# A check on softmax denominators, and a general path behind a branch at the end

## The chip, the cores and the metric

The kernel runs on one core of one Trainium2 chip. The metric is the device time of one execution in microseconds (us), the median of several runs. The core has five engines that run side by side, each with a queue of its own: TensorE (PE in the profile; PEld is its loading of weights), VectorE (DVE), ScalarE (ACT), GpSimd (POOL) and SyncE (SP). SyncE issues nearly all transfers.

## The reference

Attention over 8 batches, 12 heads, 448 positions and 64 dimensions, whose softmax has one more term in its denominator, and behind it a gate with a long convolution:

```python
scores = scale * np.matmul(q, k.transpose(0, 1, 3, 2))
m = np.max(scores, axis=-1, keepdims=True)
e = np.exp(scores - m)
attn = e / (np.sum(e, axis=-1, keepdims=True) + np.exp(-m) + 1e-09)
attn_out = np.matmul(attn, v)
...
proj = x @ w_proj            # x: the heads side by side, 448 x 768 in each batch
x1, x2, x3 = (proj[..., :D].copy(), proj[..., D:2 * D].copy(), proj[..., 2 * D:].copy())
x2_conv = np.fft.irfft(np.fft.rfft(x2, n=S, axis=1) * H, n=S, axis=1)
y = x1 * x2_conv * x3
return (y @ w_out).astype(np.float32)
```

q, k and v are normal numbers of deviation 0.1, so the scores are near 0. Without the maximum, a denominator is the sum of exp(score) over 448 keys, plus 1.

## The kernel before

The kernel computes exp(score) without subtracting the maximum, in bf16. Two heads (a head pair, 6 in a batch, 48 in all) are done at a time. `attention(i)` adds the work of head pair i: scores in four key tiles on TensorE (L772, L774), exponentials on ScalarE (L785, L791), and the product with v on TensorE (L803, L811). The matrix of v has a column of ones, so the product's last column is the denominator. `norm` on VectorE (L819 to L831) adds 1 to it, takes the reciprocal into the small tile `rec` (128 queries x 2 heads x 4 query tiles), and multiplies the product by it into `xb`. `xb` goes to `xT` by a transposing DMA (`x_dma`, L893) or, in the first batch, through TensorE (`x_pe`).

`dense(b)` adds the work behind the attention of batch b: the folds of `xT` on VectorE (L957, L962), the projection of x2 (`proj2`, L985), the transforms (L1012, L1026, L1032, L1097), the gate projections on TensorE (`gate`, L1058) whose products VectorE forms (L1073), and the output projection (`project`, L1170) with its copy on ScalarE (L1182) and the store from SyncE's queue (L1189, L1192). The dense stage of one batch runs beside the attention of later ones.

The order of every queue is set by `Plan`. Each piece of work is a task: an engine, a cost in us, a due time, what it needs and makes, and what buffers it takes and gives. `Plan.run` goes through the time of a model, lets each engine that is free start the first task in the order of due times that is ready, gives PSUM banks to those that take one, and then emits the instructions in the order found. Costs and due times are constants (`ATT`, `SLOT`, `DENSE`, `PACE` and others). Between plan times 3 and 36 gaps of TensorE are filled with idle matmuls (L1256). A task added for one engine can so alter the order on all. Nothing follows `plan.run()` but the program's end, which the profile gives as line 1335: SyncE waits for all that is out, and the engines meet twice.

```python
add("DVE", 1.03, w - 0.5, norm,
    need=[("V", i, u) for u in range(2)] + ([("X", NHP * (b - 1) - 1)] if b >= 2 else []),
    make=[("xb", i)], give=[("op", i)])
```

Of the kernel before, what the change touches and what calls it, by code (L numbers as in the profile page):

```python
# [23 lines left out]
NHP = H // 2  # L24
SCALE = 1.0 / float(np.sqrt(DH))
# [4 lines left out]
SX = 512  # L30
REM = S - 3 * 128
# [10 lines left out]
class Plan:  # L42
# [26 lines left out]
    def add(self, eng, cost, want, emit, need=(), make=(), take=(), give=(), dma=0.0, run=256, n=1, after=0.0, begun=(), late=0.0):  # L69
        self.tasks.append((want, len(self.tasks), eng, cost, emit, need, make, take, give, dma, after, run, n, begun, late))  # L70
# [186 lines left out]
def kernel(  # L257
# [11 lines left out]
    nc = tc.nc  # L269
# [20 lines left out]
    const = ctx.enter_context(tc.tile_pool(name="const", bufs=1))  # L290
# [16 lines left out]
    wproj_bf = wts.tile([128, NDT, 3 * D], BF16, name="wproj_bf")  # L307
    wout_bf = wts.tile([128, NDT, D], BF16, name="wout_bf")
    hrs = wts.tile([FQ, 2, 2, D], BF16, name="hrs")
# [24 lines left out]
    nf = nat.bitcast(F32)  # L334
# [3 lines left out]
    def stage(g, at, n):  # L338
# [4 lines left out]
    plan = Plan(  # L343
        {
            "e": 6, "er": 2, "k0": 2, "q0": 2, "u": 1, "w": 1, "xf": 1,
            "x2": 1, "xs": 2, "t0": 2, "t1": 2, "yh": 1, "g": 1, "x1": 2, "cr": 2, "cw": 1, "cv": 2, "yT": 1, "yR": 1,
            "os": 3,
        }
    )
    add = plan.add  # L350

    psum = psp.tile([128, 8 * 512], F32, name="psum")
    psum2 = psum.bitcast(BF16)
# [354 lines left out]
    W = {}  # L708
# [51 lines left out]
    def attention(i):  # L760
        b, hp = divmod(i, NHP)
# [31 lines left out]
        def out_banks():  # L793
            return pair(("op", i))[:, :, 0 : NST * (DH + 1)].rearrange("p u (n d) -> p u n d", n=NST)
# [24 lines left out]
        def norm():  # L819
            op = out_banks()  # L820
            if ("xb", b) not in W:
                W["xb", b] = xbp.tile([128, NHP, NST, 128], BF16, name="xb")
            rec = small.tile([128, 2, NST], F32, name="rec")
            nc.vector.tensor_scalar_add(rec, op[:, :, :, DH], 1.0)  # L824
            nc.vector.reciprocal(rec, rec)
            nc.vector.tensor_tensor(  # L826
                W["xb", b][:, hp].rearrange("p n (u d) -> p u n d", u=2),
                op[:, :, :, 0:DH],
                rec[:].unsqueeze(3).to_broadcast([128, 2, NST, DH]),
                op=ALU.mult,  # L830
            )  # L831
# [14 lines left out]
        for t in range(4):  # L846
            w = tau(i, t / 4 if i or t else 1.0)
            ex = with_rests(i - 1) if t == host else dict(cost=0.0, emit=lambda: None, need=[], make=[], take=[], give=[])
            if t == 0 or b == 0:

                def one(t=t, ex=ex):
# [4 lines left out]
                    need=[("kT", i), ("qT", i)] + ([("S", i - 1, 2)] if b else []) + ([] if i or t else ["kT0"]) + ex["need"]  # L856
                    + ([("S", i, t - 1) if t > 1 else ("S", i - 1, 3)] if t and (i or t > 1) else []),
                    make=[("S", i, t)] + ex["make"], take=[(ring(t), ("S", i, t))] + ex["take"], give=ex["give"])
            elif (3 * i + t) % 2 == 0:
# [3 lines left out]
                def both(pair=(old, (i, t)), ex=ex):  # L863
# [5 lines left out]
                    need=[("kT", old[0]), ("qT", old[0]), ("kT", i), ("qT", i)] + ex["need"]  # L869
                    + [("S", old[0], old[1] - 1) if old[1] > 1 else ("S", i - 1, 3)],  # L870
                    make=[("S",) + old, ("S", i, t)] + ex["make"],
                    take=[("sc", ("S",) + old), ("sc", ("S", i, t))] + ex["take"], give=ex["give"])
            add("ACT", 0.81 if t else 0.44, w - 1.0, lambda t=t: exps(t), need=[("S", i, t)],
                make=[("e", i)], take=[("e" if t else "er", (i, t))], give=[(ring(t), ("S", i, t))])
        if i == n_batches * NHP - 1:
            ex = with_rests(i)
            add("PE", 0.19 + ex["cost"], tau(i, 1.1), out_rests, need=ex["need"], make=ex["make"], take=ex["take"],
                give=ex["give"])

        w = tau(i + 1, (2 if i % 2 else 1) / 4) + 0.01  # L880
        for u in range(2):
            add("PE", 0.385, w + 0.01 * u, lambda u=u: out_rest(u), need=[("ER", i)], make=[("V", i, u)],
                take=[("op", i)], give=[("e", (i, t)) for t in range(1, 4)])
        add("DVE", 1.03, w - 0.5, norm,
            need=[("V", i, u) for u in range(2)] + ([("X", NHP * (b - 1) - 1)] if b >= 2 else []),
            make=[("xb", i)], give=[("op", i)])

        def xT():
            if ("xT", b) not in W:
# [26 lines left out]
        w = tau(i, 1.7)  # L916
        on_act = 4 <= i < 6
        old = [("G", b - 2)] if b >= 2 else []
        if b in XALL or b > 1 and hp < NHP - 1:
            if hp in (2, NHP - 1 if b in XALL else NHP - 2):  # L920
                ps = range(0, 3) if hp == 2 else range(3, hp + 1)
                add("SP", 1.3, w, x_dma, need=[("xb", NHP * b + h) for h in ps] + old,
                    make=[m for h in ps for m in (("X", NHP * b + h), ("xT", b, h))], dma=0.5 * len(ps), late=1.2)
# [309 lines left out]
                O(st, ch)  # L1233


    E = mybir.EngineType
    with (
        tc.tile_pool(name="tabs", bufs=1) as tp,
        tc.manual_schedule(engines={E.PE, E.Pool, E.DVE, E.Activation, E.SP}),
    ):  # L1240
        zero1 = tp.tile([128, 1], F32, name="zero1")
        warm = tp.tile([128, 1], F32, name="warm")
        add("DVE", 0.1, -20.0, lambda: nc.vector.memset(zero1, 0.0), make=["zero1"])
        add("POOL", 1.1, -20.0, count, make=["count"])
        add("POOL", 0.6, -19.0, lambda: make_identity(nc, ident_bf), make=["ident"])
        first = tp.tile([1, 16], BF16, name="first")
        add("POOL", 3.4, -18.5, lambda: nc.gpsimd.dma_start(first, moe_w_out[0:1, 0:16]), need=["ident"], dma=0.05)
        add("DVE", 0.2, -19.5, number, need=["count"], make=["row"])
        add("DVE", 2.6, -19.0, phases, need=["row"], make=["phases"])

        idle = tp.tile([128, 128], BF16, name="idle")
        add("DVE", 0.15, -19.9, lambda: nc.vector.memset(idle, 0.0), make=["idle"])

        def fill(i, count):
            for _ in range(count):
                nc.tensor.matmul(psum[:, 512 * i : 512 * i + 128], idle, idle)  # L1256

        plan.fill = fill

        def spin():  # L1260
# [25 lines left out]
        for b in range(n_batches):  # L1286
            if b < NSTAGED:
                staged(b)
            else:
                loaded(b)  # L1290
        add("DVE", 0.5, tau(NHP * NSTAGED) - 30.0, lambda: nc.vector.memset(kn[:, :, 0, :], 0.0),
            need=[("c" + x, g) for x in "kqv" for g in range(NHP * NSTAGED - NHP, NHP * NSTAGED - 2)], make=["zero kn"])
        for (part, ch), at in zip(LOADS, LOAD):
            if part == "F":
                add("POOL", 1.6, at, filter_load, need=["ft", "bps"], make=["filt"], take=[("yT", "F")], dma=4.1, run=1500, n=3, after=at)
            elif part == "O":
                add("POOL", 0.95, at, wout_load, make=["wout"], dma=6.9, run=1500, after=at)
            elif ch is None:
                add("POOL", 0.95, at, lambda part=part: wproj_load(part, None), make=[("w", part, 0), ("w", part, 1)], dma=6.9,
                    run=1500, after=at)  # L1300
            else:
                add("POOL", 0.7, at, lambda part=part, ch=ch: wproj_load(part, ch), make=[("w", part, ch)], dma=3.5, run=1500, after=at)
        more_tables()
        filter_spectrum()
        for i in range(n_batches * NHP):
            attention(i)
        for b in range(n_batches):
            dense(b)
        plan.run()


# [28 lines left out]
```

## Time and profile before

| what | value |
|---|---|
| time, median of 3 runs | 386.22 us (385.4 to 386.39) |
| span of the profiled execution, first to last instruction | 384.4 us |
| what lies around the span, from the three times | 1.0 to 2.0 us |
| TensorE busy | 364.9 us, 3700 matmuls |
| VectorE busy | 261.8 us, 667 instructions |
| ScalarE busy | 264.1 us, 460 instructions |
| GpSimd busy | 112.2 us, 240 instructions |
| mean granted TensorE clock | 0.998 |

The page has no other time of the profiled execution than its span, so its own time is read as the span and what the three times leave around it. A row of instructions has the line, the engine, the operation, output and input tiles, their shapes, the count, the busy time, and the idle time of the engine just before them with what ended it. A row of the windows has a stretch, its length, the busy time and count of TensorE, weight loads, VectorE, ScalarE and GpSimd, then the granted clock, the share of the DMA engines, and GB/s. A row of waits has who waited for whom, the sum, the number of times and the longest. A q behind an engine's name is its queue. An issue of a DMA is on its queue's engine; its landing is later.

### The profile page before, as it was taken

What the parts mean: (1) busy time and instruction counts of PE and PEld (TensorE: products, weight loads), DVE (VectorE), ACT (ScalarE), POOL (GpSimd) and SP (SyncE); (2) the same over time, 40 slices, a digit from 0 to 9 for tenths busy, and PEclk for the clock granted to TensorE, in tenths of its full rate; (3) what the DMA queues carried; (4) which work ended last, traced back from release to release, by engine and by line L of the source; (5) the groups of instructions that cost most, each with busy time, mean ns of one, the idle gap of its engine ahead of it and who ended that gap; (6) DMA issues with size and microseconds to landing.
All of it is one profiled execution on the core that took longest, in us unless ns stands there. A gap on an engine that the chain in (4) does not pass through costs nothing.

```text
span 384.4 us, 9536 instructions
## 1 busy us (share of the span) xinstructions
PE 364.9 (95%) x3700; PEld 232.4 (60%) x3700; DVE 261.8 (68%) x667; ACT 264.1 (69%) x460; POOL 112.2 (29%) x240
## 2 busy tenths in 40 slices
PE   7887799999998999889989999999999999999995
PEld 6555575557654676545755666565665567667553
DVE  6575758996868357997596576665488725987660
ACT  5698487884885868767756658886778587444543
POOL 5692436141835533445552411110000000000000
PEclk9999999999999999999999999999999999999999
DMA  8999998599999999999999933592302132200214
GB/s 207 265 225 232 249 219 197 131 178 218 262 269 273 249 261 244 263 230 251 247 241 226 274 112 100 102 210 96 84 3 43 41 124 43 43 1 2 82 41 165
DMA packets 116333, 64.43 MB, mean 168 GB/s; under 512 B 73085, under 2 KB 112704, under 8 KB 116288
## 3 DMA queue, kind: packets, MB, share of 16 engines
q1 hardware_dynamic: 111568, 58.18, 63.5%
q0 software_dynamic: 4480, 5.41, 8.3%
q8 instruction: 29, 0.48, 0.5%
q10 hardware_dynamic: 240, 0.23, 0.3%
q14 instruction: 16, 0.13, 0.1%
HBM read 43.86 MB, written 11.01 MB: 143 GB/s over the span
## 4 chain that ended last, share of the span: by engine, by line
PE 65%; DVE 13%; DMA 12%; ACT 4%; issue 2%; POOL 2%; SPq 2%; POOLq 0%; DVEq 0%; ACTq 0%
PE psum L1058 19%; PE psum L985 14%; PE psum L1170 12%; PE psum L811 6%; PE psum L772 5%; DMA nat<-in_k_dram 5%; DMA xT<-xb 3%; DVE t L1026 2%; DMA nat<-in_v_dram 2%; PE psum L1097 2%; PE psum L1012 2%; DMA nat<-in_q_dram 2%; DVE xf L962 2%; DVE yh L1032 2%; ACT e L785 2%
## 5 line engine op out<-in xcount | busy, mean ns | idle before, releaser
L785 ACT ACTIVATE e<-psum 128x896 bf16<-128x896 f32 x144 | 126.4, 925 | 21.8 <-PE psum L772 21.6
L1058 PE MATMUL psum<-xT,wproj_bf 128*128 128x448 bf16 x576 | 122.4, 352 | 0.1
L1058 PEld LDWEIGHTS <-wproj_bf 128*128 128x128 bf16 x576 | 53.5, 97 | 42.8 <-issue 1.3
L985 PE MATMUL psum<-wproj_bf,xf 128*113 128x384 bf16 x384 | 69.1, 326 | 1.5 <-DVE g L1073 0.7
L985 PEld LDWEIGHTS <-xf 128*113 128x113 bf16 x384 | 50.0, 132 | 15.3 <-issue 3.4
L1170 PE MATMUL psum<-wout_bf,yT 128*128 128x384 bf16 x288 | 52.9, 326 | 0.0
L811 PE MATMUL psum<-vn,e 128*128 128x65 bf16 x1152 | 44.7, 194 | 0.0
L1070 ACT CAST x<-psum 128x448 bf16<-128x448 f32 x48 | 25.6, 534 | 25.8 <-PE psum L1058 24.5
L1026 DVE TENSOR_TENSOR t<-xs,hrs 113x768 bf16<-113x768 bf16 (+1 forms) x64 | 37.0, 613 | 8.0 <-ACT xs L1020 8.0
L772 PE MATMUL psum<-qT,kT 64*128 64x448 bf16 x288 | 40.8, 355 | 0.6 <-ACT kT L485 0.4
L1182 ACT COPY osb<-psum 128x384 f32<-128x384 f32 x56 | 26.4, 484 | 21.3 <-PE psum L1170 20.0
L811 PEld LDWEIGHTS <-e 128*128 128x128 bf16 x1152 | 39.2, 97 | 2.8
L568 POOL CAST nat<-nat 112x512 bf16<-112x512 f32 x36 | 24.1, 671 | 52.6 <-DMA nat<-in_q_dram 49.2
L1170 PEld LDWEIGHTS <-yT 128*128 128x128 bf16 x288 | 27.5, 98 | 19.2 <-issue 1.5
L824 DVE TENSOR_SCALAR rec<-psum 128x8 f32<-128x8 f32 x48 | 7.7, 161 | 44.8 <-PE psum L811 44.3
L1073 DVE TENSOR_TENSOR g<-x,psum 128x448 bf16<-128x448 bf16 x48 | 29.5, 615 | 11.9 <-PE psum L1058 9.5
L999 ACT CAST x<-psum 113x384 bf16<-113x384 f32 x32 | 15.5, 483 | 28.7 <-PE psum L985 28.5
L826 DVE TENSOR_TENSOR xb<-psum,rec 128x512 bf16<-128x512 f32 x48 | 33.2, 691 | 1.7
L1020 ACT CAST xs<-psum 113x384 bf16<-113x384 f32 (+1 forms) x64 | 28.2, 499 | 3.8 <-PE psum L1012 3.6
L1106 ACT CAST cr<-psum 128x452 bf16<-128x452 f32 x48 | 25.3, 547 | 7.0 <-PE psum L1097 6.6
L791 ACT ACTIVATE er<-psum 128x448 bf16<-128x448 f32 x48 | 26.7, 556 | 4.6 <-PE psum L774 4.6
L997 DVE CAST x<-psum 113x384 bf16<-113x384 f32 x32 | 17.5, 550 | 14.1 <-PE psum L985 14.1
(111 smaller groups left out, 435.7 us busy)
## 6 DMA issues: line engine op xcount, KB each, us to landing
nat<-in_q_dram SPq DMA_DIRECT2D x47, 224.0 KB, 4.7
out_dram<-osb SPq DMA_DIRECT2D x24, 384.0 KB, 2.4
nat<-in_k_dram SPq DMA_DIRECT2D x41, 192.0 KB, 4.9
nat<-in_v_dram SPq DMA_DIRECT2D x41, 192.0 KB, 4.9
wproj_bf<-in_moe_w_proj_dram POOLq DMA_DIRECT2D x2, 1152.0 KB, 17.3
rests<-in_k_dram SPq DMA_DIRECT2D x8, 192.0 KB, 4.9
rests<-in_v_dram SPq DMA_DIRECT2D x8, 192.0 KB, 5.2
out_dram<-osb SPq DMA_DIRECT2D x8, 192.0 KB, 2.9
```

Of the source, the lines that this page charges most:

```text
L772: nc.tensor.matmul(sc[:, u, 0:S], kT[b % 2][c, hp, t, :], qT[b % 2][c, hp, :])
L785: nc.scalar.activation(to, of, AF.Exp, scale=SCALE)
L791: nc.scalar.activation(to, of, AF.Exp, scale=SCALE)
L811: nc.tensor.matmul(out_bank(u)[:, n, :], P["e"][1 + t][:, u * S + n * 128 : u * S + n * 128 + 128], vn[b % 2][:, hp, 4 * u + t, :], start= ...
L826: nc.vector.tensor_tensor(W["xb", b][:, hp].rearrange("p n (u d) -> p u n d", u=2), op[:, :, :, 0:DH], rec[:].unsqueeze(3).to_broadcast([1 ...
L985: nc.tensor.matmul(pps[:FQ, :DCH], W["xf", b][:, pg, kt, 0:FQ], wproj_bf[:, kt, D + ch * DCH : D + (ch + 1) * DCH], start=(kt == 0), stop= ...
L1020: nc.scalar.copy(L["xs", par, ch][:K, pg % 2, :], L["Z", pg, ch][:K, :DCH])
L1026: nc.vector.tensor_tensor(t[:K], L["xs", par, ch][:K], h, op=ALU.mult)
L1058: nc.tensor.matmul(p[:, :S], wproj_bf[:, kt, 2 * part * D + dt * 128 : 2 * part * D + (dt + 1) * 128], xT()[:, kt, 0:S], start=(kt == 0), ...
L1073: nc.vector.tensor_tensor(g[:, dt, :], L["x1", dt], p[:, :S], op=ALU.mult)
L1170: nc.tensor.matmul(ops[:n, :DCH], y[:, dt, 0:n], wout_bf[:, dt, ch * DCH : (ch + 1) * DCH], start=(dt == 0), stop=(dt == NDT - 1),)
L1182: nc.scalar.copy(L["os", st][:n, ch * DCH : (ch + 1) * DCH], L["O", st, ch][:n, :DCH])
```

## The change

`norm` writes the denominators' reciprocals into a buffer of the batch (`dens`, one of two) that is kept. After the last head pair of a batch VectorE takes the minimum of it with `low`, a running minimum that starts at 1. After all batches, `judge` reduces `low` over its free axis and compares it with 1/65536; a matmul with a column of ones sums the 128 marks, and VectorE copies the sum to `flag` as an integer. All of these are tasks of the plan. Behind `plan.run()` the flag is loaded into a register of each engine, and where it is over 0 a general path (`stable`) recomputes the attention with the maximum in f32 for each batch, and `dense` runs again for it with a plan of its own. No constant of the planner is altered.

```diff
--- before.py
+++ after.py
@@ -349,6 +349,13 @@
     )
     add = plan.add
 
+    LARGE = 65536.0
+    dens = [const.tile([128, NHP, 2, NST], F32, name=f"den{i}") for i in range(2)]
+    low = const.tile([128, NHP, 2, NST], F32, name="low")
+    one = const.tile([128, 1], BF16, name="one")
+    bad = const.tile([128, 1], BF16, name="bad")
+    flag = const.tile([1, 1], I32, name="flag")
+
     psum = psp.tile([128, 8 * 512], F32, name="psum")
     psum2 = psum.bitcast(BF16)
 
@@ -820,7 +827,7 @@
             op = out_banks()
             if ("xb", b) not in W:
                 W["xb", b] = xbp.tile([128, NHP, NST, 128], BF16, name="xb")
-            rec = small.tile([128, 2, NST], F32, name="rec")
+            rec = dens[b % 2][:, hp]
             nc.vector.tensor_scalar_add(rec, op[:, :, :, DH], 1.0)
             nc.vector.reciprocal(rec, rec)
             nc.vector.tensor_tensor(
@@ -882,8 +889,11 @@
             add("PE", 0.385, w + 0.01 * u, lambda u=u: out_rest(u), need=[("ER", i)], make=[("V", i, u)],
                 take=[("op", i)], give=[("e", (i, t)) for t in range(1, 4)])
         add("DVE", 1.03, w - 0.5, norm,
-            need=[("V", i, u) for u in range(2)] + ([("X", NHP * (b - 1) - 1)] if b >= 2 else []),
+            need=[("V", i, u) for u in range(2)] + ([("X", NHP * (b - 1) - 1), ("low", b - 2)] if b >= 2 else []),
             make=[("xb", i)], give=[("op", i)])
+        if hp == NHP - 1:
+            add("DVE", 0.12, w + 3.0, lambda: nc.vector.tensor_tensor(low, low, dens[b % 2], op=ALU.min),
+                need=[("xb", NHP * b + h) for h in range(NHP)] + ["low"], make=[("low", b)])
 
         def xT():
             if ("xT", b) not in W:
@@ -1232,6 +1242,78 @@
             for ch in range(2):
                 O(st, ch)
 
+
+    def watch():
+
+        def fresh():
+            nc.vector.memset(low, 1.0)
+            nc.vector.memset(one, 1.0)
+
+        def judge():
+            worst = small.tile([128, 1], F32, name="worst")
+            nc.vector.tensor_reduce(worst, low[:].rearrange("p g u n -> p (g u n)"), axis=mybir.AxisListType.X, op=ALU.min)
+            nc.vector.tensor_single_scalar(bad, worst, 1.0 / LARGE, op=ALU.is_lt)
+
+        last = ("low", n_batches - 1)
+        hy = ("hy", "flag")
+        add("DVE", 0.15, 20.0, fresh, make=["low"], after=12.0)
+        add("DVE", 0.35, tau(NHP * n_batches, 4.0), judge, need=[("low", b) for b in range(n_batches)], make=["bad"])
+        add("PE", 0.1, tau(NHP * n_batches, 4.0), lambda: nc.tensor.matmul(bank(hy)[0:1, 0:1], bad, one), need=["bad"],
+            make=["count bad"], take=[hy])
+        add("DVE", 0.1, tau(NHP * n_batches, 4.0), lambda: nc.vector.tensor_copy(flag, bank(hy)[0:1, 0:1]), need=["count bad"],
+            make=["flag"], give=[hy])
+
+    def stable(b):
+
+        at = [0]
+
+        def room(*shape):
+            n = int(np.prod(shape[1:]))
+            t = nf[0 : shape[0], at[0] : at[0] + n]
+            at[0] += n
+            return t.rearrange("p (a c) -> p a c", a=shape[1]) if len(shape) > 2 else t
+
+        eye = room(128, 128)
+        qa, ka, va = (room(SP, NST, DH) for _ in range(3))
+        qt, kt = (room(DH, S) for _ in range(2))
+        ex, et = room(128, S), room(SP, NST, 128)
+        top, neg, off, den = (room(128, 1) for _ in range(4))
+        area = [psum[:, 512 * i : 512 * i + 512] for i in range(8)]
+        nc.vector.tensor_copy(eye, ident_bf)
+        W["xb", b] = x = xbp.tile([128, NHP, NST, 128], BF16, name="xb")
+        W["xT", b] = xt = xtp.tile([128, NDT, SX], BF16, name="xT")
+        nc.vector.memset(x[:, :, NST - 1, :], 0.0)
+        for h in range(H):
+            hp, u = divmod(h, 2)
+            for to, of in ((qa, q), (ka, k), (va, v)):
+                nc.sync.dma_start(to, of[b, h].rearrange("(t p) d -> p t d", p=SP))
+            for i, (of, to) in enumerate(((qa, qt), (ka, kt))):
...
+            for n in range(NST):
+                m = 128 if n < 3 else REM
+                sc = area[2][0:m, 0:S]
+                nc.tensor.matmul(sc, qt[:, n * 128 : n * 128 + m], kt)
+                nc.vector.tensor_reduce(top[0:m], sc, axis=mybir.AxisListType.X, op=ALU.max)
+                nc.vector.tensor_scalar(neg[0:m], top[0:m], -SCALE, None, op0=ALU.mult)
+                nc.scalar.activation(ex[0:m], sc, AF.Exp, scale=SCALE, bias=neg[0:m])
...
+        for hp in range(NHP):
+            for t in range(NST):
+                nc.tensor.transpose(psum2[:, 1024 * 5 + t * 128 : 1024 * 5 + (t + 1) * 128], x[:, hp, t, :], ident_bf)
+            nc.vector.tensor_copy(xt[:, hp, 0:S], psum2[:, 1024 * 5 : 1024 * 5 + S])
 
     E = mybir.EngineType
     with (
@@ -1306,7 +1388,24 @@
             attention(i)
         for b in range(n_batches):
             dense(b)
+        watch()
         plan.run()
+
+    overflow = nc.values_load(flag[0:1, 0:1], min_val=0, max_val=128)
+    with (
+        tc.If(overflow > 0),
+        tc.manual_schedule(engines={E.PE, E.Pool, E.DVE, E.Activation, E.SP}),
+    ):
+        W.clear()
+        for b in range(n_batches):
+            stable(b)
+            plan = Plan(plan.size)
+            plan.FILL, add = (0.0, 0.0, 0.0), plan.add
+            ready = ["ft", "bt", "half", "wout", ("hrs", 0), ("hrs", 1), ("y", b - 1, 1)]
+            ready += [("w", n, i) for n in range(3) for i in range(2)] + [("xT", b, h) for h in range(NHP)]
+            add("DVE", 0.01, -100.0, lambda: None, make=ready, after=1.0)
+            dense(b)
+            plan.run()
 
 
 # ---- launch: one core; inputs and outputs as the reference has them ----
```

More of the change, by code (lines that the diff above doesn't have):

```diff
@@ new lines, in stable @@
+    def stable(b):
[21 more added lines that the diff above has]
+                for t in range(NST):
+                    nc.tensor.transpose(area[i][0:DH, t * SP : (t + 1) * SP], of[:, t, :], eye[0:SP, 0:SP])
+                nc.vector.tensor_copy(to, area[i][0:DH, 0:S])
+            for n in range(NST):
[5 more added lines that the diff above has]
+                nc.scalar.activation(ex[0:m], sc, AF.Exp, scale=SCALE, bias=neg[0:m])
+                nc.vector.tensor_scalar(off[0:m], neg[0:m], 88.0, None, op0=ALU.min)
+                nc.scalar.activation(off[0:m], off[0:m], AF.Exp)
+                nc.vector.tensor_reduce(den[0:m], ex[0:m], axis=mybir.AxisListType.X, op=ALU.add)
+                nc.vector.tensor_scalar(den[0:m], den[0:m], off[0:m, 0:1], 1e-9, op0=ALU.add, op1=ALU.add)
+                nc.vector.reciprocal(den[0:m], den[0:m])
+                nc.vector.tensor_scalar(ex[0:m], ex[0:m], den[0:m, 0:1], None, op0=ALU.mult)
+                for t in range(NST):
+                    nc.tensor.transpose(area[3][0:SP, t * 128 : t * 128 + m], ex[0:m, t * SP : (t + 1) * SP], eye[0:m, 0:m])
+                nc.vector.tensor_copy(et[:, :, 0:m], area[3][0:SP].rearrange("p (a c) -> p a c", a=NST)[:, :, 0:m])
+                for t in range(NST):
+                    nc.tensor.matmul(area[4][0:m, 0:DH], et[:, t, 0:m], va[:, t, :], start=(t == 0), stop=(t == NST - 1))
+                nc.scalar.copy(x[0:m, hp, n, u * DH : (u + 1) * DH], area[4][0:m, 0:DH])
+        for hp in range(NHP):
+            for t in range(NST):
+                nc.tensor.transpose(psum2[:, 1024 * 5 + t * 128 : 1024 * 5 + (t + 1) * 128], x[:, hp, t, :], ident_bf)
+            nc.vector.tensor_copy(xt[:, hp, 0:S], psum2[:, 1024 * 5 : 1024 * 5 + S])
```

## The prediction

> **What bounds the kernel now.** I read the summary of engines first, then the windows by stage, then what TensorE waited for, and last the final microseconds.
>
> ```profile
> PE 364.9 (95%) x3700; PEld 232.4 (60%) x3700; DVE 261.8 (68%) x667; ACT 264.1 (69%) x460; POOL 112.2 (29%) x240
> PE   7887799999998999889989999999999999999995
> ```
>
> TensorE is busy for 364.9 of 384.4 us. VectorE has 122.6 us of idle time, so small work on it costs nothing unless TensorE waits for its result. The windows say where TensorE's idle time lies:
>
> ```profile
> 24.00:36.00 12.00, 9.89 (x173) 7.09 (x173) 9.31 (x28) 11.07 (x18) 6.14 (x14) 1.00 1.17 228
> 36.00:50.00 14.00, 10.62 (x131) 7.57 (x130) 9.15 (x25) 8.40 (x12) 6.28 (x11) 1.00 1.17 242
> 150.00:200.00 50.00, 45.95 (x471) 28.04 (x470) 40.54 (x92) 35.21 (x61) 24.80 (x50) 1.00 1.07 249
> 250.00:300.00 50.00, 50.00 (x535) 31.43 (x532) 32.71 (x90) 38.74 (x67) 1.18 (x3) 1.00 0.35 84
> 330.00:360.00 30.00, 30.00 (x188) 19.08 (x187) 24.49 (x66) 13.32 (x29) 0.00 (x0) 1.00 0.11 28
> 360.00:385.00 25.00, 20.53 (x136) 11.91 (x134) 9.18 (x24) 10.40 (x22) 0.00 (x0) 0.95 0.26 95
> ```
>
> The second number is TensorE's busy time in the stretch. From 250 us to the last matmul at 380.56 TensorE is full. It has holes in the first 50 us, and 4.05 us of them between 150 and 200 us. Those last ones come from VectorE; the view of waits, cut to that stretch and engine, names them:
>
> ```profile
> PE psum L1097 <- DVE g L1073: 2.9, 3, 1.2
> PE psum L985 <- DVE g L1073: 0.7, 1, 0.7
> PE psum L803 <- DVE g L1073: 0.5, 1, 0.5
> ```
>
> The end is the part that the change touches most. The timeline of SyncE's queue has the last store; the view of line 1335 (the program's end) has what follows it; the view of line 1189 has the time that a store takes:
>
> ```profile
> 381.07 0.34 SPq L1189 DMA_DIRECT2D out_dram<-osb  x1
> ```
>
> ```profile
> L1335 SPq EVENT_SEMAPHORE  x11: 17/28/28, 381.5 to 384.4; - x11
> L1335 SPq DRAIN  x3: 7/7/7, 383.6 to 383.9; - x3
> L1335 ACTq EVENT_SEMAPHORE  x2: 17/17/17, 383.8 to 384.4; - x2
> ```
>
> ```profile
> DMA to landing us min/median/max: 2.3/2.4/5.5
> ```
>
> So the last store is issued by 381.4, lands 2.3 us after its start (381.07 + 2.3 = 383.4), SyncE's queue drains at 383.6, and two rounds in which the engines meet end the span at 384.4. Closing costs 0.8 us behind the drain, and one round some 0.2 us (drain at 383.6, the others released at 383.8).
>
> The program itself is fetched while it runs, and the page shows it:
>
> ```profile
> q8 instruction: 29, 0.48, 0.5%
> q14 instruction: 16, 0.13, 0.1%
> ```
>
> One packet of q8 is 0.48 MB / 29, some 16 KB, and takes 0.5% x 384.4 x 16 / 29 = 1.06 us; one of q14 is 8 KB and takes 0.1% x 384.4 x 16 / 16 = 0.4 us (0.2 to 0.6 by the rounding).
>
> The sum is made against the profiled execution, whose span is 384.4 us. The three timed runs lie 1.0 to 2.0 us above that span, their median 386.22 us 1.8 us above; I add the change in span to the median. About 0.3% (1.16 us) is what a measurement of this kernel can tell from no change.
>
> **The change part by part.**
>
> Denominators kept in "dens" instead of "rec": the same three instructions with the same shapes (161, 203 and 691 ns at lines 824 to 826). 0.
>
> Eight minima on VectorE, 128x48 f32: nearest rows are the 128x8 f32 TENSOR_SCALAR of 161 ns and the 128x128 bf16 TENSOR_TENSOR of 268 ns (L1141); I take 0.22 us, 1.8 us in all. They lie in VectorE's 122.6 us of idle time. Each stands behind the last normalisation of its batch, so "xb", which the transposing DMA waits for, is not later; what queues behind a minimum is the next copy or gate product. Where that is a product that TensorE waits for (150 to 200 us, line 1073), a minimum moves the matmul by 0.22 us: two batch ends there, at most 0.4 us. I take 0.1.
>
> The two memsets at about 12 us: 59 ns each by the row of "zero", beside 5.2 us of idle VectorE in 12 to 24 us. 0. Without that cover they would cost 0.12.
>
> The judgement: a reduction (about 0.22 us), a comparison (0.15, as the 128x1 TENSOR_SCALARs of L652), and the copy of the flag out of PSUM (0.17, as L824). VectorE is free for 5.5 of the 30 us from 330 on. The reduction waits for the last minimum, in VectorE's own order, so nothing new is late. The copy waits for the one-column matmul; behind it in the queue stand the products of batch 7, delayed by a semaphore's turn of some 0.2 us.
>
> The one-column matmul stands in TensorE's full stretch, so all of its time counts: 24 matmuls of L811 with 65 columns take 0.87 us in the chain of waits, 0.04 each; the longest row for one from start to end is 0.19. I take 0.1. It also waits for "bad", and behind it in TensorE's queue stand the gate matmuls of the last batch (L1058). After 250 us the trace shows no wait of TensorE for VectorE to speak of, but the longest one anywhere for a VectorE result is 1.23 us. So 0.04 to 1.4, taken 0.1.
>
> The planner: new VectorE tasks shift the due times of everything that it sorts from plan time 12 on, and so the orders of all queues. Not shown by any row. Bounds: the 4.05 us of holes from 150 to 200 us close (a gain of 4.1), or as many again open (a loss of 4.1). With TensorE full from 250 us on, any order does the same work, so I take 0 and keep both ends.
>
> The end. Five queues each read the flag into a register, compare, and jump over the general path, which is thousands of instructions long (12 heads x 4 query tiles x some 20 instructions, for 8 batches). None of this is in the trace, so it is bounded.
> Read and compare: below by two queue instructions (0.06 each from one closing wait to the next: 11 of them in the 0.65 us around a landing), above by a store's round trip of 2.3. It is one word, so nearest to what a queue spends on one instruction with addresses, the 0.34 us DMA issue; with the compare I take 0.5.
> The jump: below 0.06 if the target is already there; above a round trip of 2.3 and a 16 KB block of 1.06, 3.4. All that is known of fetching is that a block is a DMA. The 384 KB store moves for some 0.95 us of its 2.4 (about 400 GB/s in its window), so 1.4 us is not transfer; with 0.4 to 1.06 for the block that is 1.8 to 2.5. I take 2.0.
> [...]
> Semaphores: the path not taken must leave them as the other path would, bounded by 0 and by two passes of the closing waits; one pass, 11 x 0.06, is 0.6, which I take.
> Meeting: if the engines meet before the branch (the last store landed, 383.4 and a round of 0.2), nothing of this hides under the store. If they do not, it runs under the 2.0 us between 381.4 and 383.4. I take the meeting, since the general path writes what the fast path still reads, and price its round 0.2; and one more pass of closing waits of 0.4 that no longer hides under the landing.
> Sum of the end: 0.5 + 2.0 + 0.6 + 0.2 + 0.4 = 3.7 us.
>
> Total: 0.1 + 0.1 + 3.7 = 3.9: span 388.3, time 386.2 + 3.9 = 390.1 us, slower by 1.0%. Chance of this forecast, with its own range of 388.7 to 392: 0.43.
>
> **The rivals.**
>
> No meeting: each queue branches when its own work is done. TensorE, VectorE and GpSimd are done by 380.6 and hide everything. SyncE is free at 381.4; 0.5 + 2.0 + 0.6 brings it to 384.5, then 0.6 of waits and 0.8 of closing make 385.9. That is 1.5 more than 384.4, with 0.2 for the rest 387.9 us. For it: nothing in the data needs a meeting when the path is not taken. Chance 0.26.
>
> Hidden, no change: as before, but jump and read together cost SyncE under 2.0 us, the block being there or coming in 0.4. Then only the 0.6 and 0.2 remain: 386.2 to 387.2 us. [...] Chance 0.10.
>
> Faster: the new order closes the holes of 150 to 200 us (L1097, L985 and L803 waiting for the product of L1073). All 4.05 us closed with the unmet end of 1.5 gives 386.2 - 4.05 + 1.7 = 383.9 us. It decides from 2.9 us closed on with that end, and can't with my 3.7. Against it: new tasks on VectorE give it more to do in just that stretch (40.5 of 50 us busy). Chance 0.05.
>
> New waits: the changed order opens 4 us of holes, in the first 50 us or where VectorE is late with a product. 390.1 + 4.1 = 394.2 us. For it: in the first 50 us TensorE is idle 9.3 us and waits for casts, key and query copies and "xb", all of them in queues that the planner reorders. Chance 0.15.
>
> The branch is taken: the eight dense stages run again, whose L1058, L985 and L1170 alone hold 122.4 + 69.1 + 52.9 = 244 us of TensorE, so over 630 us. Denominators are sums of 448 exponentials of numbers near 0, far below 65536. Chance 0.01.
>
> **How the numbers follow.** The prediction is the likeliest, 390.1. The range goes from 386.9 (below the unmet end and the upper edge of the hidden one) to 394.5 (the new waits); out of it fall the faster case, most of the hidden one, and the upper tail, some 0.17. Slower by over 0.3%: 0.43 + 0.26 + 0.15 + 0.01 = 0.85. Within 0.3%: 0.10. Faster: 0.05.
>
> **What would show it.** The end: in the rows of the last 10 us, reads and branches of all five queues behind the landing of the last store, and 3 us or so between branch and closing (met), or between 381 and 384 (unmet). Instruction packets in the last 5 us, one for each engine, show the fetch. The minima: eight of 0.2 us. The matmul: no gap behind it in TensorE's timeline. The planner: TensorE's busy sum stays at 365, and the last matmul's end moves from 380.56 by under 1 us; if that end moves by more, the change's cost is order and not branch, and the forecast is wrong in its reason even where its number holds. A last matmul near 380.7 with a span of 385 would say that the branch hides.

## The result and the profile after

The changed kernel took 390.09 us in the median of 15 runs, against 386.22 before. The ratio to before is 1.0097, with a 95% interval of 1.0074 to 1.0120, so about 3.7 us (2.9 to 4.6) slower. The ratios here leave out executions more than 1.5% above the fastest of their kernel. A second comparison of the same kernel, told below, gave 1.0118 (1.0058 to 1.0179). The forecast was 390.1 us, slower; its reason holds only in part, as told below.

The summary of engines and the windows of the changed kernel, with the same columns as before:

```profile
PE 364.7 (95%) x3701; PEld 232.4 (60%) x3701; DVE 264.6 (69%) x680; ACT 264.3 (69%) x460; POOL 111.5 (29%) x240
```

```profile
150.00:200.00 50.00, 47.28 (x487) 29.01 (x485) 42.03 (x99) 35.62 (x63) 24.14 (x48) 1.00 1.10 248
250.00:300.00 50.00, 50.00 (x504) 30.80 (x502) 33.75 (x95) 37.67 (x66) 0.00 (x0) 1.00 0.31 73
330.00:360.00 30.00, 30.00 (x192) 19.25 (x192) 23.20 (x63) 13.60 (x30) 0.00 (x0) 1.00 0.11 28
360.00:386.00 26.00, 18.27 (x120) 10.55 (x118) 8.66 (x22) 8.83 (x19) 0.00 (x0) 0.94 0.28 95
```

TensorE does one matmul more, VectorE 13 instructions and 2.8 us more. TensorE is full from 250 us on as before, and its holes from 150 to 200 us are still there (2.7 us in this execution). TensorE's waits in the main part are mostly for the same producers as before, and not longer in sum: it is idle for 13.6 us up to its last matmul, against 15.6 before. The end has a new wait. This is the view of what SyncE's queue waited for from 376 us on:

```profile
SPq L1396 <- SPq L1396: 4.3, 1, 4.3
SPq L1434 <- PEq L1434: 0.7, 2, 0.5
```

In the kernel before, the same view has the landing of the store in that place:

```profile
SPq L1335 <- DMA out_dram<-osb: 1.5, 2, 1.0
```

Line 1396 is the branch. SyncE's queue stands still there for 4.3 us, and waits for nothing but itself. The timeline of its queue has the last store, and the views of lines 1394 (the load of the flag), 1396 and 1434 (the closing) show the rest:

```profile
378.81 0.34 SPq L1199 DMA_DIRECT2D out_dram<-osb  x1
```

```profile
L1394 SPq TENSOR_LOAD <-flag x1: 1205/1205/1205, 330.5 to 330.5; - x1
L1394 ACTq TENSOR_LOAD <-flag x1: 673/673/673, 378.3 to 378.3; - x1
```

```profile
L1396 SPq EVENT_SEMAPHORE  x8: 17/17/17, 383.5 to 384.0; - x8
...
L1396 DVEq COMPARE_BRANCH  x1: 72/72/72, 371.9 to 371.9; - x1
L1396 DVEq EVENT_SEMAPHORE  x1: 21/21/21, 374.7 to 374.7; - x1
L1396 PEldq COMPARE_BRANCH  x1: 3426/3426/3426, 375.8 to 375.8; - x1
L1396 ACTq COMPARE_BRANCH  x1: 50/50/50, 379.1 to 379.1; - x1
L1396 SPq COMPARE_BRANCH  x1: 58/58/58, 379.2 to 379.2; - x1
...
L1396 ACTq EVENT_SEMAPHORE  x1: 17/17/17, 383.5 to 383.5; - x1
```

Read it engine by engine, from COMPARE_BRANCH to the EVENT_SEMAPHORE behind it. VectorE branches at 371.9 and goes on at 374.7: 2.8 us. ScalarE branches at 379.05 and goes on at 383.52: 4.4 us behind the branch. SyncE branches at 379.20, and its first instruction past the general path is at 383.51: 4.3 us. GpSimd, which has no work in the general path, goes on 0.13 us behind its branch at 331.8. TensorE's branch takes 3.4 us, but at 375.8 it has that much work queued, and its matmuls run on to 378.27 and hide most of it. The packets of the instruction queues lie in these gaps. The view of DMA queues, cut to 379.2 to 383.5 us:

```profile
q8 instruction: 1, 0.02, 1.3%
q14 instruction: 2, 0.02, 0.9%
```

The two packets of q14, 8 KB each, start 1.8 to 1.9 us behind the branches (381.00 and 381.01), take 0.31 and 0.32 us, and another 2.2 us pass before the two queues go on.

It is best to measure the end from the start of the last store, since the main part of one execution is up to some us longer than that of another. Before: 381.07 to 384.43, a tail of 3.37 us. After: 378.81 to 385.74, 6.93 us. The difference, 3.56 us, is 0.92%, which is all but 0.05% of the measured ratio. The spans alone (384.4 and 385.7) would give 1.3 us, because the profiled execution after had its last store 2.3 us earlier; the next experiment shows that the change has no part in that.

One reason why main parts differ can be read from the traces. In some executions TensorE's granted clock falls to 0.5 for one stretch of 3.4 us within the main part. The kernel without the branch, told next, has one from 39.3 to 42.7 us; its window of 38 to 44 us, with the granted clock as the last number but two, shows it (0.28 of 6 us is 3.4 us at half the clock):

```profile
38.00:44.00 6.00, 4.57 (x51) 3.41 (x52) 3.76 (x9) 2.27 (x3) 4.67 (x9) 0.72 1.14 260
```

Of the 14 traces told here, eight have such a stretch (one of them two), and their last store starts at 381.6 to 382.5 us. The other six, with those of the kernel before and of the changed kernel among them, have none, and it starts at 378.8 to 381.2 us. What sets the spread within the six is not shown.

### The profile page after: what moved, and what is told of

It reads as the page before. It is cut to its first block, busy times and chain, and to the rows that moved or that the text cites. A ratio compares the mean times of both kernels' runs of the same rounds, so it can differ in the third digit from the quotient of the medians.

```text
span 385.7 us, 9576 instructions
## 1 busy us (share of the span) xinstructions
PE 364.7 (95%) x3701; PEld 232.4 (60%) x3701; DVE 264.6 (69%) x680; ACT 264.3 (69%) x460; POOL 111.5 (29%) x240
## 4 chain that ended last, share of the span: by engine, by line
PE 54%; DMA 22%; DVE 8%; SPq 7%; POOL 4%; issue 2%; ACT 1%; POOLq 0%; DVEq 0%
PE psum L1068 17%; PE psum L995 12%; PE psum L1180 11%; DMA nat<-in_k_dram 10%; DMA nat<-in_q_dram 10%; PE psum L818 5%; PE psum L779 4%; SPq L547 3%; PE psum L1107 2%; DVE t L1036 2%; PE psum L1022 2%; DVE yh L1042 1%; DMA xT<-xb 1%; SPq L569 1%; PE psum L781 1%
## 5 line engine op out<-in xcount | busy, mean ns | idle before, releaser
L1036 DVE TENSOR_TENSOR t<-xs,hrs 113x768 bf16<-113x768 bf16 (+1 forms) x64 | 36.1, 599 | 7.3 <-ACT xs L1030 7.3
L818 PEld LDWEIGHTS <-e 128*128 128x128 bf16 x1152 | 39.3, 97 | 2.8
L831 DVE TENSOR_SCALAR den<-psum 128x8 f32<-128x8 f32 x48 | 7.8, 162 | 45.2 <-PE psum L818 44.5
L833 DVE TENSOR_TENSOR xb<-psum,den 128x512 bf16<-128x512 f32 x48 | 33.2, 692 | 1.7
```

Of the source, the lines that this page charges most:

```text
L818: nc.tensor.matmul(out_bank(u)[:, n, :], P["e"][1 + t][:, u * S + n * 128 : u * S + n * 128 + 128], vn[b % 2][:, hp, 4 * u + t, :], start= ...
L833: nc.vector.tensor_tensor(W["xb", b][:, hp].rearrange("p n (u d) -> p u n d", u=2), op[:, :, :, 0:DH], rec[:].unsqueeze(3).to_broadcast([1 ...
L1036: nc.vector.tensor_tensor(t[:K], L["xs", par, ch][:K], h, op=ALU.mult)
```

## The experiments

The tail is everywhere the time from the start of the last store to the end of the span.

**The work without the branch.** From the changed kernel:

```diff
         watch()
         plan.run()
 
-    overflow = nc.values_load(flag[0:1, 0:1], min_val=0, max_val=128)
-    with (
-        tc.If(overflow > 0),
...
```

> The changed kernel with the minima, the judgement, the matmul and the copy of the flag, but without the load of the flag into registers, the branch and the general path behind it. Theory (the end costs all: SyncE's and ScalarE's jumps over the general path, and a longer closing): 386.2 us, the time before, within 0.8, since the orders of the queues are the same but for the added tasks. Rival (the new tasks and the altered order cost it): 388 us or more. Rival (the new work speeds the plan up by 2 us, as the earlier last matmul of the one profile of the changed kernel would have it): 384.2 us.

Measured: 1.0013 of before (0.9983 to 1.0044), tail 3.37 us, exactly that of before. The view of waits of SyncE's queue has the store's landing again as the longest wait of the end, as before:

```profile
SPq L1419 <- DMA out_dram<-osb: 1.5, 2, 1.0
```

Laid side by side with the kernel before, by operation and shape, the work and the DMA issues of ScalarE, GpSimd and SyncE stand in the same order. TensorE's list is the same but for the flag's matmul. VectorE's is the same but for the 13 added instructions up to the 585th of its 667; behind that, a fold and a gate product of the last batch change places. So the planner moved next to nothing, and the 13 instructions cost nothing that can be measured (at most 0.44% by the interval). Both rivals fall, the one that sees a 2 us faster plan as well.

**The branch without the work.** The normalisation before is kept, and the minima are gone (these lines of the edit are left out here); the flag is set by a memset:

```diff
...
-        watch()
         plan.run()
+        nc.vector.memset(flag, 0)
 
     overflow = nc.values_load(flag[0:1, 0:1], min_val=0, max_val=128)
```

> The kernel before with its own normalisation and no judgement; the flag is set to 0 by one memset on VectorE behind its last work, and then the flag is loaded, compared and the same general path jumped over as in the changed kernel. Theory (the end costs all): 386.2 + 3.5 to 4 = 390 us, as the changed kernel, with its wider scatter too. Rival (the new tasks cost it): 386.2 to 387 us.

Measured: 1.0136 (1.0090 to 1.0181), tail 6.44 us; SyncE's jump took 3.8 us, ScalarE's 4.4, VectorE's 2.8. The branch alone costs what the change costs, within the two intervals, and the rival falls. The tail accounts for 0.8% of the 1.36%.

**A near target.** The general path is five instructions, one for each engine:

```diff
-        W.clear()
-        for b in range(n_batches):
-            stable(b)
...
+        nc.vector.memset(low, 1.0)
+        nc.gpsimd.memset(one, 1.0)
+        nc.scalar.copy(dens[0], dens[1])
+        nc.tensor.matmul(psum[0:1, 0:1], bad, one)
+        nc.sync.dma_start(out[n_batches - 1, 383:384, 0:48], dens[0][0:1].rearrange("p g u n -> p (g u n)"))
```

> The changed kernel with a general path of five instructions, one for each engine, in place of the thousands; the condition is the same and the path is not taken. This leaves the recomputation out. Theory (the jump waits for its target to be fetched, 4.3 us on SyncE in the profile of the changed kernel): with a near target the jump takes 0.1 us, SyncE is at its last waits before the store has landed, and the time is 386.2 + 0.5 to 1.0 = 387 us. Rival (a branch costs this wherever it goes, or it is loading the flag): 389 to 390 us.

> The kernel with a general path of five instructions once more (it leaves the recomputation out). Its first comparison gave 1.0057 of before, with a tail (start of the last store to the end of the span) of 3.39 us, the same as before. Theory (only the tail costs): 0.999 to 1.003 of before. Rival (loading and judging the flag costs time that no row of the tail shows): 1.004 to 1.008 again.

Measured: 1.0057 (1.0022 to 1.0092) the first time and 1.0003 (0.9966 to 1.0040) the second, and a tail of 3.39 us both times. The view of the branch's line in the second:

```profile
L1396 ACTq COMPARE_BRANCH  x1: 45/45/45, 382.8 to 382.8; - x1
L1396 SPq COMPARE_BRANCH  x1: 57/57/57, 382.9 to 382.9; - x1
L1396 ACTq EVENT_SEMAPHORE  x1: 17/17/17, 383.0 to 383.0; - x1
L1396 SPq EVENT_SEMAPHORE  x1: 17/17/17, 383.1 to 383.1; - x1
```

SyncE is past the branch 0.2 us after it, and the store's landing ends the kernel as before. So load, comparison and branch are free here, and it is the far target that costs. The first ratio, 388.4 us, lies 1.4 us above the theory's 387, and its interval reaches into the rival's range; the second excludes the rival. I take the tail, which is the same in both, and leave the 1.0057 as unexplained.

**The general path placed aside.**

```diff
-        tc.If(overflow > 0),
+        tc.If(overflow > 0, preferred_fallthrough_block=False),
```

> The changed kernel with the general path placed aside, so that the path not taken goes on behind the comparison and only the taken one jumps to the general path. Theory (the far jump costs it): if the end of the program lies near too, 387 us; if the end lies behind the general path, one far jump is left, later by the closing semaphores, and the time is 390 us or more; SyncE's rows behind the comparison say which. Rival (the comparison, not the distance): 389 to 390 us with no stall behind the semaphores.

Measured: 1.0205 (1.0154 to 1.0256), tail 8.65 us. Behind the comparison SyncE goes on after some 0.1 us and counts its semaphores, the last ones behind the store's landing, and then a second branch at 384.26 leads to the program's end, which lies behind the general path:

```profile
L1396 SPq COMPARE_BRANCH  x2: 38/50/61, 380.2 to 384.3; - x2
```

```profile
L1434 SPq EVENT_SEMAPHORE  x14: 17/28/28, 386.8 to 388.4; - x14
```

That jump takes 2.5 us (384.30 to 386.80), with the store landed and no data moving; two packets of instructions are all that the DMA engines carry. The far jump was only moved to a place where nothing hides it. ScalarE's second branch, at 380.28, jumps beside the last store and takes 3.3 us, less than the 4.4 of the changed kernel. Of 2.05%, the tail has 1.4%; the rest has no row.

**The changed kernel again.**

> The changed kernel once more, for a second trace of its end and a second comparison. Theory (the far jumps of SyncE and ScalarE): from the start of the last store to the end of the span 6.4 to 7 us, as 6.93 and 6.44 in the two traces with a far jump, against 3.37 without one; jumps of 3.8 to 4.5 us while the store moves, VectorE's 2.8 us before it; time 1.007 to 1.012 of before. Rival (chance in one trace): another tail, below 5 us.

Measured: 1.0118 (1.0058 to 1.0179), tail 7.00 us, jumps of 4.3 us (SyncE), 4.5 (ScalarE) and 2.9 (VectorE). The end repeats itself.

**A hint.** A line in front of the load, and a label on the branch:

```diff
+    tc.mark_branch_hint_location("general", hint="LikelyTaken", engines=[E.SP, E.Activation])
     overflow = nc.values_load(flag[0:1, 0:1], min_val=0, max_val=128)
...
-        tc.If(overflow > 0),
+        tc.If(overflow > 0, label="general"),
```

> The changed kernel with a prefetch hint (the branch is likely taken, past the general path) for SyncE's and ScalarE's branches, which the compiler puts at the start of their queues. Theory (the jump waits for the fetch of its target): if the hint fetches the target ahead, the jumps fall below 0.5 us, the tail to 4.2 us or less and the time to 387 to 388 us; if a hint so far ahead does nothing, all is as in the changed kernel, 389 to 391 us. Rival (the jump's cost is not the fetch): the instruction packets come earlier, the jumps stay at 4 us.

Measured: 1.0106 (1.0047 to 1.0165), tail 5.69 us. The view of the branch's line:

```profile
L1397 ACTq COMPARE_BRANCH  x1: 68/68/68, 382.4 to 382.4; - x1
L1397 SPq COMPARE_BRANCH  x1: 78/78/78, 382.6 to 382.6; - x1
L1397 ACTq EVENT_SEMAPHORE  x1: 17/17/17, 382.9 to 382.9; - x1
```

The two jumps fall from 4.3 and 4.4 us to 0.47 and 0.42 (VectorE, without a hint, stays at 2.8), though in the program as built the hint is the kernel's first instruction on either queue, and the branches come at 382.4 and 382.6 us. The packets go with them: from ScalarE's branch on, q14 has four packets in the changed kernel and two here, and neither of the two lies in the short jumps. So the long jumps have packets of q14 in their gaps and the short ones none, which I read as the fetch of the target. When the hinted target came is not shown: up to that branch q14 moved 18 packets in either kernel.

The kernel gains only 1.2 us in the tail, not the 2.7 or more that the theory asks, and the ratio shows no gain over the changed kernel. The last store now sets the end and lands 3.8 us after its start, not 2.3, and 2 semaphores and 12 closing waits of 0.06 us follow that landing.

**SyncE's target near, and the last copies on VectorE.** The general path's transfers are issued from GpSimd's queue (the first diff, one place of three; `again` is filled only where the general path is built), which has nothing at the end; in the second kernel the last store's two copies out of PSUM go to VectorE as well:

```diff
-                nc.sync.dma_start(out[b, st * 128 : (st + 1) * 128, :], osb)
+                (nc.gpsimd if again else nc.sync).dma_start(out[b, st * 128 : (st + 1) * 128, :], osb)
```

```diff
-            nc.scalar.copy(
+            last = not again and b == n_batches - 1 and st == 2
+            (nc.vector.tensor_copy if last else nc.scalar.copy)(
```

> The changed kernel with the general path's transfers on GpSimd's queue, so that SyncE has nothing to jump over; ScalarE still jumps far. Theory: SyncE's branch costs 0.14 us as with the short path, ScalarE's still 4.4 us, which begins 0.24 us behind the last store's issue and so ends the kernel: tail 4.7 + 0.2 + 0.8 = 5.7 us, 1.2 less than in the changed kernel; time 388.5 to 389.5. Rival (only SyncE's jump counts): tail 3.4 to 4 us, time 387.

> As the kernel with the general path's transfers on GpSimd's queue, and the last two copies out of PSUM (the last store's two halves) on VectorE, so that ScalarE jumps some 1.9 us before the last store, and VectorE after its copy. Theory: the last engine that jumps sets the end, now VectorE: load of the flag 0.55, branch, and a jump of 2.8 us (no contention) to 4.4 us (while the store moves), so a tail of 4.4 to 6.1 us; time 387.5 to 389.5. Rival (only ScalarE's jump is long): tail 3.4 to 4 us, 387 us or less.

Measured: 1.0062 (1.0024 to 1.0101) with a tail of 5.69 us, and 1.0084 (1.0049 to 1.0119) with 5.61 us. In the first SyncE's jump is 0.14 us and ScalarE's 4.4 ends the kernel, as the theory has it. In the second ScalarE jumps early and takes 2.8 us, and VectorE, which now jumps while the last store moves, takes 4.0. It goes on 4.3 us after the store's start, and the store lands 0.2 us later still and ends the kernel, which the theory did not have. VectorE's queue pays 2.8 us where its packet moves before the last stores do (372.90 to 373.36 us in the changed kernel, whose last stores start from 373.67 on), and 4.0 beside the last store, so about 1.2 us of a late jump goes with the store's traffic.

**A general path for one batch.**

```diff
         W.clear()
-        for b in range(n_batches):
+        for b in range(1):
             stable(b)
```

> The changed kernel with a general path for the first batch alone (it leaves the other seven out of the recomputation), so that SyncE's part of it is some 40 instructions, ScalarE's 160 and VectorE's 450, while TensorE's and the program stay long. Theory (a jump waits when its target lies outside what is fetched ahead): SyncE's jump 0.14 us, VectorE's 2.8 us as before, ScalarE's between; if ScalarE's is near, a tail of 3.4 to 4.2 us. Rival (the jump's cost grows with the distance): VectorE's jump falls well below 2.8 us. For the stores, which land 3.0 to 3.3 us after their start in all kernels with the general path and 2.4 us in those without: 2.4 to 2.6 us if the program's length is what matters.

Measured: 1.0108 (1.0049 to 1.0168), tail 5.65 us. SyncE's jump over some 40 instructions takes 0.46 us, ScalarE's over some 160 takes 4.4 as over 1260, VectorE's 2.8 as over eight times as many. From ScalarE's 160 instructions to its 1260 the cost didn't grow with the distance, and the rival falls. The theory's 0.14 us for SyncE is missed: 0.46 us over some 40 instructions lies between the near jump and the far one, and no row says why. ScalarE's jump ended the kernel, not the store: some 160 instructions are already far, at 4.4 us.

**A general path that stores nothing.**

```diff
...
             osb = L["os", st]
+            if again:
+                return
             if st < 3:
...
```

> The changed kernel with a general path that doesn't store its result (it leaves out the 32 stores of the recomputation). Theory on the slow stores (they land 3.0 to 3.3 us after their start in all kernels with the general path, 2.4 us without): if a second writer of the output is what slows them, 2.4 us; if it is the length of the program, 3.0 us or more. The jumps of SyncE and ScalarE stay at 3.8 to 4.5 us and the time at 1.007 to 1.012 of before; a store that lands earlier changes nothing there, since SyncE's jump ends later than the store's landing.

Measured: 1.0168 (1.0110 to 1.0226), tail 8.12 us: more than with the stores, which no theory had. The jumps are as they were (3.9 us on SyncE, 4.4 on ScalarE), but behind the first of its 12 closing waits SyncE stands still once more, from 386.73 to 388.22, with packets of instructions at 386.64 and 386.95. The view of line 1439, the closing of this kernel, has the beginning and end of it:

```profile
L1439 SPq EVENT_SEMAPHORE  x14: 17/28/28, 386.7 to 389.8; - x14
```

The 14 take 1.6 us in the changed kernel (384.1 to 385.7) and 3.1 here. What SyncE waits for in that second stop is not shown by any run. Of this kernel's stores of 384 KB, the median lands 2.9 us after its start and the last 3.2, so a second writer isn't needed to slow them; what that median says is told at the end.

**Both remedies.**

```diff
+    tc.mark_branch_hint_location("general", hint="LikelyTaken", engines=[E.Activation])
     overflow = nc.values_load(flag[0:1, 0:1], min_val=0, max_val=128)
```

> Both remedies: the general path's transfers on GpSimd's queue, so that SyncE's jump is near (0.14 us in the trace of that kernel), and a prefetch hint for ScalarE's branch (0.42 us in the trace of the kernel with hints). Theory: no jump is late any more, and the last store's landing sets the end again; it landed 2.3 us after its start in kernels without the general path and 3.4 to 3.9 us in two with it, so with 0.4 for the waits behind it and 1.0 for the closing the tail is 3.7 to 5.3 us, and the time 1.001 to 1.006 of before. Rival (the hint doesn't reach a branch alone): ScalarE's jump at 4.4 us, tail 5.7, 1.006 of before or more.

Measured: 1.0057 (1.0017 to 1.0096), tail 5.39 us, 0.1 above the range. ScalarE's jump took 0.42 us, SyncE's 0.14. The store's landing ends the kernel alone, as the waits of SyncE's queue say:

```profile
SPq L1438 <- DMA out_dram<-osb: 3.2, 2, 2.7
```

It came 4.3 us after the store's start. This version keeps the general path at some 0.6 of the change's price, by the tail (2.0 of 3.6 us) and by the ratio; it doesn't beat the kernel before.

## Why the prediction was right, and where it was not

**The total.** 390.1 us forecast, 390.09 measured. The sum of the end, 3.7 us, met 3.56 and 3.63 in the two traces. That it met them so closely is luck: the jump was taken too short, the meeting and the load of the flag were taken as costs and are none, and these errors cancelled. What held is that the price is the far jump at the end and not the new work.

**"Meeting": wrong.** No engine meets another before the branch. GpSimd branches at 331.8 us, VectorE at 371.9, TensorE at 375.8, each when its own work is done. The structure is the one that the first rival had (chance 0.26). So the 0.2 of a round was not there, and the jump ran beside the store from 379.2 on.

**"The jump": mis-sized.** Taken as 2.0 us, bounded by 3.4; measured 4.3 on SyncE and 4.4 on ScalarE. VectorE's jump, whose packet moves before the last stores do, keeps to the bound: 2.8 us, of which the packet is 0.46 (it starts 1.0 us behind the branch, and 1.4 us pass behind it). What the bound left out is the last store. Beside it SyncE's packet starts 1.8 us behind its branch in place of 1.0, and 2.2 us pass behind it in place of 1.4.
Packets of the instruction queues lie in the gaps, and SyncE's 4.3 us becomes 0.2 with a near target and 0.5 with a hint.
The comparison itself is short where a queue goes on behind it: with the path placed aside, some 0.1 us passes from the first branch to the next instruction on ScalarE, VectorE and SyncE. Over the near target it is 0.18 to 0.23 us, over a far one 2.5 to 4.5.

**"Read and compare": placed wrong.** 0.5 us taken; the load takes 0.5 to 1.2 us, but SyncE's stands at 330.5 us in a queue that is idle then, and only ScalarE's 0.67 is late. Free for SyncE.

**"Semaphores": right; the closing waits: short.** 0.6 taken for the semaphores, 383.51 to 384.11 measured for eight on SyncE. The closing waits are 12 and take 0.74, where I had 0.4 that no longer hides.
With the meeting's 0.2 and the load's 0.5 gone, 2.3 more for the jump, 0.3 more for the closing waits, and some 1.9 us hidden under the store, the sum is what it was: from the last store's start 0.4 to the branch, 4.3 for the jump, 0.6, 0.7, and 0.9 to close, 6.9.

**The work: right.** The eight minima took 0.20 us five times and 0.41 to 0.56 three times (0.22 taken), 2.4 us in all, and nothing waits for them. The matmul took 0.16 us from start to end, and the next gate matmul starts 0.09 us after it:

```profile
330.00 0.16 PE L1261 MATMUL psum<-one,bad 128*1 128x1 bf16 x1
330.09 1.12 PE L1068 MATMUL psum<-xT,wproj_bf 128*128 128x448 bf16 x5
```

**"The planner", 0 of between -4.1 and 4.1: right.** The orders are the same, so the faster rival and the rival of new waits had no mechanism; they deserved less than the 0.20 that I gave the two. By the prediction's own sign the reason would be order and not branch, since the last matmul's end moved from 380.5 to 378.3 us in the changed kernel's first trace. The sign was a bad one: with the work and no branch it is at 381.1, in the second trace of the changed kernel at 381.2, so one execution differs from the next by more than the 1 us that the sign allowed.

**The branch is not taken**, as forecast.

**What stays open.** In every comparison the ratio is above what the tail gives, by 0.02% (SyncE near) to 0.68% (the path aside). In three the difference is beyond the interval: the path aside, the branch alone (0.56%), and the near target the first time (0.56%). Each tail is from one execution, and no row shows more. The 0.46 us over 40 instructions, the second stop of the kernel without stores and the way of the hint are open as well.

## What to carry to other kernels

In this kernel a path that is never taken costs at the place where the queues jump over it. Its price is not in the condition (SyncE goes on 0.2 us behind its branch over a near target) but in the far target (4.3 us). On ScalarE it was 4.4 us over some 160 instructions as over 1260, and it is paid in full by the queues that jump last: here at the end of the program, by the one with the last store (SyncE, 4.3 us) and the one that fills it (ScalarE, 4.4 us). Before placing such a path, ask for each queue what still covers its jump (here TensorE's queued matmuls and VectorE's early end), keep the path's instructions off the queue that has no cover (SyncE's jump took 0.14 us then), or give that branch a hint (ScalarE's took 0.42); and where only the end changes, compare the tails and not the spans.

## What was not expected

A jump took longer beside traffic: VectorE 2.8 us before the last stores move and 4.0 beside the last one, SyncE 2.5 with no data moving and 3.8 to 4.3 beside it, ScalarE 2.8 early and 3.3 to 4.5 beside it. The last store lands later in turn. In the changed kernel and in the one with both remedies a 16 KB packet of instructions runs for 0.9 to 1.0 us from 2.2 us behind the store's start, and the store's last three packets start about when it ends: the last is done at 3.7 to 3.8 us where it is done at 2.0 without a far jump.

A hint worked from 382 us ahead: the hinted jumps took 0.47 us on SyncE and 0.42 on ScalarE.

Stores of 384 KB land 2.9 to 3.3 us after their start, in the median of 24, in all kernels with a far jump, and 2.4 us in those without (before, the work without the branch, the near target). A path of one batch has 3.1. The median misleads: it is not so during the whole run. In every kernel eleven of the first twelve stores land after some 3.2 us or more. They lie before 250 us, where the windows have a DMA share of 0.68 to 1.12; later it is 0.35 or less, and most stores land after 2.3. With the two groups so even, two or three slower stores carry the median from one to the other, and they are the last ones. The view of the stores' line in the changed kernel has this for the stores from 240 to 372 us:

```profile
DMA to landing us min/median/max: 2.3/2.3/4.7
```

and this for the three from 372 us on:

```profile
DMA to landing us min/median/max: 2.7/2.9/4.2
```

The kernel before has 2.3/2.3/4.6 and 2.3/2.3/2.3 there. So the slow stores are those at the end, in the time when the queues jump and packets of instructions move. In the kernel whose VectorE jumps last, where no packet of q14 falls into the first two of the three, these land after 2.31 and 2.35 us as before, and the third, beside VectorE's jump, after 4.5. That the packets are what slows them fits these traces, but no run varied the packets alone. While SyncE's jump ends later than the landing this costs nothing; with a hint the landing, 3.8 us after the store's start and 4.3 with both remedies, is what is left.
